# A chunked linear-attention and token-mixing kernel: values per unit, two transposes by DMA, decays as they are, one sum for X, another order

## The chip, the cores and the metric

The kernel runs on one core of one Trainium2 chip. A core has five engines that run beside each other: TensorE (PE), VectorE (DVE), ScalarE (ACT), GpSimd (POOL) and SyncE (SP), which here only issues DMA transfers. The metric is the device time of one execution in microseconds. Runs of the kernel before took 100.32 to 101.12 us, median 100.91 of 3.

## The reference

Inputs r, k, v, w have the shape (batch 4, heads 8, sequence 768, head size 48), u is 8 x 48. First a linear attention with a decay per channel, then a token mixer over the 384 channels of all heads:

```python
for t in range(S):                                   # for each batch and head
    cur = outer(u * k[t], v[t])
    y[t] = r[t] @ (state + cur)
    state = w[t][:, None] * state + outer(k[t], v[t])
# x: y with the heads side by side, (4, 768, 384)
wq = x @ w_q;  wk = x @ w_k                          # to 64 columns
W_tok = einsum('bsd,btd->bst', wq, wk) / 8
out = relu(einsum('bst,btd->bsd', W_tok, x)) @ w_out
```

## The kernel before

The sequence is cut into **units** of 256 positions, three to a batch, so there are 12 units, 0 to 11; units 9 to 11 are the last batch. A unit has two **chunks** of 128 positions, c = 0 and 1. Within a chunk the recurrence is done by matrix products: with the running product of the decays, r is multiplied by it (RT) and k divided by it (KT), the product of both, masked, gives the attention inside the chunk (AM), and a state per head (SB) carries over to the next chunk.

The program is a list of **steps**, each with a name, a unit and sometimes a chunk. For one unit they are, with the engine that can do them in brackets (E is PE, D is DVE, A is ACT, P is POOL, S is SP's DMA queue):

- wg, kg, rg, vg (S): the loads of w, k, r, v, 384 KB each.
- ln (A): logarithm of the decays. k16, r16, v16 (P, A or D): casts to bf16.
- cw (E): running sums of the logarithms. ep, en (A): their exponentials with plus and with minus.
- kT, rT (E): transposes of k and r. ks (A or D): kT copied out of PSUM. qT (D): rT times ks. RT (D): rT times ep. KT: ks times en, on POOL (P) or DVE (D), or straight from PSUM on DVE (written d).
- vp (E), VB (A or D): the values brought into the order of the partitions. dps (E), dd (A or D), Vd (P or D): the bonus term with u.
- A (E), AM (D): RT times KT for eight heads, then the mask. kb (E), kd (A or D): KT turned back.
- sn (E), SB (D): the new state. In form c the product goes out in two halves of 64 columns.
- yi, ya (E): y from the old state and from inside the chunk. X (D): y plus the bonus term, the row of the mixer's input.
- xt (E), XT (A or D): X transposed and copied out. qk (E), QK (A): X times w_q and w_k. In unit 11 X, xt, XT run per chunk, and qk is split into wq and wk with the copies wqc and wkc.

After the third unit of a batch: T (E), TS (A), the product of QK and X over the batch; then for each unit of the batch mx (E), rl (A or D, relu), fp (E, times w_out), os (A or D, copy out of PSUM) and st (a DMA store). The steps z are matmuls on zeros that keep PE's clock up; `WARM` counts them, and `setup` issues more before the first step.

The order of the steps over all engines is written out by hand in `ORDER` (found by a search), the engine of each step with a choice in `WAYS`, the PSUM banks in `BANKS`. Each engine does its own steps strictly in that order; a step waits by semaphores for those it depends on. Loads and stores are issued by SP in the same order, and a load waits until its buffer (`RINGS`, mostly 2 or 4 deep) is free.

Two things of the last batch differ from the others before the change. Its values are loaded at once for all three units (`WHOLE`, `load_whole`, the tile vw), in four transfers whose pieces are the 192 bytes of one position, straight into the right partitions; v16 and vp fall away there and VB is a cast from vw on POOL. And all decays are centred: a constant MU is taken off each logarithm, and the tables gx, gv, gk, IDU and a scaled mask US bring the factors back, in X, kd, sn and AM.

Of the kernel before, what the change touches and what calls it, by code (L numbers as in the profile page):

```python
# [142 lines left out]
def kernel(  # L143
# [81 lines left out]
    pos0 = const([C, 1], I32, "pos0")
    pos1 = const([C, 1], I32, "pos1")
    gx = const([C, 1], F32, "gx")
    gv = const([C, 1], F32, "gv")
    gk = const([C, 1], F32, "gk")
# [664 lines left out]
```

## Time and the profile before

| | |
|---|---|
| runs of the kernel before | 101.12, 100.32, 100.91 us (median 100.91) |
| the profiled execution | 101.37 us, of which the span of the trace is 99.6 |
| instructions in the span | 4492 |
| busy in the span | PE 86.6, DVE 84.9, ACT 79.0, POOL 69.5 us |
| moved by DMA | 24.68 MB, mean 248 GB/s |
| granted TensorE clock | 1.00 |

How the views are read: *busy* is the time in which an engine executes, without its waits. The view of stretches gives the busy time of each engine between two moments, the granted clock, the share of the DMA engines and what they moved. In the groups of instructions a line has the kernel's line, the engine, the operation, the tiles out<-in with their shapes, the count, the busy time in us and the mean of one in ns; behind the next bar the idle time of the engine just before these instructions, and what ended it. In the timeline each line begins with start and length in us. The chain that ended last is followed backwards from the last instruction, at each step to what released it. PSUM tiles all bear the name PS.

### The profile page before, as it was taken

How to read it: one execution, taken by the hardware profiler on the slowest of the kernel's cores; microseconds unless marked ns; L12 is line 12 of the kernel's file. 1: busy time of each engine (PE TensorE's matmuls, PEld its weight loads, DVE VectorE, ACT ScalarE, POOL GpSimd, SP SyncE). 2: the span in 40 equal slices, each digit the busy share in tenths (PEclk: the TensorE clock that was granted, in tenths of full speed). 3: DMA queues.
4: the chain of work that ended last, by engine and by line, in shares of the span. 5: the costliest groups of instructions: out<-in, count | busy, mean ns of one | idle time of the engine just before them, and what ended most of it. 6: DMA issues, size and time to landing. Idle time of an engine off the chain costs nothing.

```text
span 99.6 us, 4492 instructions
## 1 busy us (share of the span) xinstructions
PE 86.6 (87%) x1906; PEld 63.3 (64%) x1911; DVE 84.9 (85%) x154; ACT 79.0 (79%) x135; POOL 69.5 (70%) x82
## 2 busy tenths in 40 slices
PE   5978796879886998999999999889998999999930
PEld 1325473756774767777776777759787687776610
DVE  6284999799979999979999999999999799783740
ACT  6034998799996799899999998999899766666920
POOL 6866354999799895799999989498996392500000
PEclk9999999999999999999999999999999999999999
DMA  1999999799999999999999977998993056030794
GB/s 17 313 327 349 324 337 296 195 295 335 289 314 298 225 311 329 344 321 268 271 330 305 316 114 218 251 156 201 282 417 115 7 210 264 10 158 7 277 367 149
DMA packets 45141, 24.68 MB, mean 248 GB/s; under 512 B 31552, under 2 KB 43968, under 8 KB 45120
## 3 DMA queue, kind: packets, MB, share of 16 engines
q1 hardware_dynamic: 44960, 24.19, 84.0%
q8 instruction: 15, 0.25, 0.9%
q10 hardware_dynamic: 160, 0.20, 0.5%
q14 instruction: 6, 0.05, 0.1%
HBM read 19.66 MB, written 4.72 MB: 245 GB/s over the span
## 4 chain that ended last, share of the span: by engine, by line
PE 37%; DVE 23%; SPq 20%; DMA 7%; issue 7%; ACT 3%; ACTq 0%; DVEq 0%
PE PS L179 37%; SPq L232 9%; SPq L237 8%; DMA vg<-in_v_dram 7%; DVE AM L595 7%; DVE X L710 6%; DVE RT L516 3%; SPq L355 2%; DVE qT L506 2%; DVE ks L333 2%; DVE SB L658 1%; ACT VB L327 1%; SPq L357 1%; ACT MX L339 1%; DVE kd L335 1%
## 5 line engine op out<-in xcount | busy, mean ns | idle before, releaser
L595 DVE TENSOR_TENSOR AM<-PS,US 128x1024 bf16<-128x1024 f32 x24 | 28.8, 1218 | 0.7 <-PE PS L179 0.7
L526 POOL TENSOR_TENSOR KT<-ks,en 128x1024 bf16<-128x1024 bf16 (+1 forms) x10 | 19.7, 1965 | 4.7 <-DVE ks L333 3.3
L575 POOL TENSOR_TENSOR Vd<-VB,dd 128x768 bf16<-128x768 bf16 (+1 forms) x14 | 18.1, 1293 | 4.5 <-ACT dd L327 3.4
L454 ACT ACTIVATE en<-PS 128x1024 bf16<-128x1024 f32 (+1 forms) x14 | 12.5, 907 | 3.0 <-PE PS L179 2.9
L179 PEld LDWEIGHTS <-KT 48*128 48x128 bf16 (+1 forms) x312 | 9.7, 94 | 6.6 <-issue 4.5
L447 ACT ACTIVATE ep<-PS 128x512 bf16<-128x512 f32 (+1 forms) x28 | 13.7, 555 | 0.1
L179 PE MATMUL PS<-wo,MX 128*128 128x384 bf16 x72 | 13.5, 327 | 0.0
L710 DVE SCALAR_TENSOR_TENSOR X<-PS,gx,Vd 128x384 bf16<-128x384 f32 x22 | 12.5, 609 | 0.7 <-PE PS L179 0.6
L407 ACT ACTIVATE lw<-wg 128x768 bf16<-128x768 f32 x12 | 10.3, 857 | 2.9 <-DMA wg<-in_w_dram 2.9
L179 PE MATMUL PS<-RT,KT 48*128 48x128 bf16 x192 | 9.7, 218 | 1.2 <-ACT VB L327 0.4
L327 ACT COPY os<-PS 128x768 f32<-128x768 f32 (+1 forms) x11 | 7.9, 714 | 3.5 <-PE PS L179 3.5
L418 POOL CAST k<-kg 128x768 bf16<-128x768 f32 x10 | 8.3, 827 | 2.5 <-DMA kg<-in_k_dram 2.5
L179 PE MATMUL PS<-Z 128*128 128x512 bf16 x25 | 8.4, 461 | 1.4 <-DVE Z L250 1.2
L418 POOL CAST r<-rg 128x768 bf16<-128x768 f32 x10 | 8.2, 825 | 1.6 <-DMA rg<-in_r_dram 1.6
L179 PEld LDWEIGHTS <-MX 128*128 128x128 bf16 x72 | 6.5, 97 | 3.6 <-DVE MX L341 0.2
L516 DVE TENSOR_TENSOR RT<-PS,ep 128x1024 bf16<-128x1024 bf16 (+1 forms) x14 | 8.4, 605 | 0.0
L179 PE MATMUL PS<-VB,AM 128*128 128x48 bf16 x192 | 8.0, 184 | 0.4 <-issue 0.4
L506 DVE TENSOR_TENSOR qT<-PS,ks 128x1024 bf16<-128x1024 bf16 x12 | 8.2, 684 | 0.1
L339 ACT ACTIVATE MX<-PS 128x768 bf16<-128x768 f32 (+1 forms) x12 | 8.0, 682 | 0.4
L179 PE MATMUL PS<-CM,lw 64*128 64x128 bf16 x192 | 7.4, 217 | 0.5 <-DVE AM L595 0.3
L327 ACT CAST VB<-PS 128x768 bf16<-128x768 f32 x8 | 6.4, 804 | 1.1 <-PE PS L179 0.6
L179 PEld LDWEIGHTS <-AM 128*128 128x128 bf16 x192 | 6.3, 96 | 1.6 <-issue 0.7
(90 smaller groups left out, 191.9 us busy)
## 6 DMA issues: line engine op xcount, KB each, us to landing
kg<-in_k_dram SPq DMA_DIRECT2D x12, 384.0 KB, 6.4
wg<-in_w_dram SPq DMA_DIRECT2D x12, 384.0 KB, 5.0
rg<-in_r_dram SPq DMA_DIRECT2D x12, 384.0 KB, 5.8
vg<-in_v_dram SPq DMA_DIRECT2D x9, 384.0 KB, 6.3
out_dram<-os SPq DMA_DIRECT2D x9, 384.0 KB, 2.5
vw<-in_v_dram SPq DMA_DIRECT2D x4, 288.0 KB, 6.7
out_dram<-os SPq DMA_DIRECT2D x5, 192.0 KB, 2.4
wof<-in_moe_w_out_dram SPq DMA_DIRECT2D x1, 576.0 KB, 6.2
```

What stands on the lines that cost most here:

```text
L179: return nc.tensor.matmul(o, l, rr, start=start, stop=stop, skip_group_check=True, is_transpose=trans)
L327: nc.scalar.copy(o, i)
L407: nc.scalar.activation(view(lw.tile, 0, [[64, H], [512, 2], [1, D]]), view(g["wg"].tile, 0, [[D2, H], [D, 2], [1, D]]), ACT.Ln, bias=0.0, ...
L418: op(view(o.tile, 0, [[64, NP], [256, 4], [1, D]]), view(g[src].tile, 0, [[2 * D2, NP], [D, 4], [1, D]]))
L447: nc.scalar.activation(view(ep.tile, cs[0] * NP * EW + off, [[EW, NP * len(cs)], [step, 2], [1, 32]]), view(at(cw), cs[0] * 512 + j * 64, ...
L454: nc.scalar.activation(en.tile[:, ds(cs[0] * 512, w_)], at(cw)[:, ds(cs[0] * 512, w_)], ACT.Exp, bias=0.0, scale=-1.0)
L506: lambda e: nc.vector.tensor_tensor(plain(qT.tile), turned(512), plain(ks.tile), ALU.mult),
L516: nc.vector.tensor_tensor(plain(RT.tile, cs, 32), turned(512, cs, True), plain(ep.tile, cs, EW // 4), ALU.mult)
L526: x.tensor_tensor(KT.tile[:, cols], ks.tile[:, cols], en.tile[:, cols], ALU.mult)
L575: (nc.vector if e == "D" else nc.gpsimd).tensor_tensor(Vd.tile[:, cols], VB.tile[:, cols], view(dd.tile, cs[0] * H, [[1, len(cs) * H], [0, ...
L595: AMs[c] = add(("AM", n, c), "D", lambda e, c=c, A=A: nc.vector.tensor_tensor(view(AM[c].tile, 0, [[C, 8], [1, C]]), view(at(A), 0, [[C, 8 ...
L710: nc.vector.scalar_tensor_tensor(view(X.tile, 2 * i * DM + hh * D, [[D2, H], [1, D]]), view(at(y), hh * 512, [[D, H], [1, D]]), gx, view(V ...
```

## The change

- **Values.** The last batch's values are loaded, cast and brought in order per unit, as in the other batches (`WHOLE = ()`): three loads vg of 384 KB in place of four vw of 288 KB, three v16, three vp, and VB copied from PSUM.
- **Decays not centred.** MU, gx, gv, gk, IDU and the scaling of US go, with eight iotas and five small operations of the setup. kd becomes a plain copy; sn takes the identity.
- **X as one sum.** With gx gone, X of units 0 to 10 is one tensor_tensor of 768 columns in place of two scalar_tensor_tensor of 384. In unit 11 each of the two becomes a tensor_tensor.
- **XT of units 9 and 10 by DMA** (`TURN`). In place of xt (six 128x128 transposes, or twelve halves, on PE) and the copy XT, SP issues one DMA that transposes X from SBUF to SBUF (step xs). qk waits for it. The ring of XT gets a third buffer.
- **Order.** `ORDER`, `WAYS` and `BANKS` come from a new search. `begin` lets either of yi and ya come first. Three more z and three more warming matmuls in the setup.

```diff
@@ class Buf
+        self.begun = set()
+    def begin(self, part=None):
+        new = part not in self.begun
+        self.begun.add(part)
+        return new
...
-WARM = 12
+WARM = 15
+TURN = (9, 10)
...
-    WHOLE = (B - 1,)
-    SHIFT = 25
-    MU = -SHIFT * math.log(2.0) / C
-    UNIT = 2.0 ** -SHIFT
+    WHOLE = ()
...
-        SB=(4, NP * D, BF16), XT=(2, 2 * DM, BF16), ...
+        SB=(4, NP * D, BF16), XT=(3, 2 * DM, BF16), ...
...
@@ setup
-        for _ in range(18):
+        for _ in range(21):
             mm(PS[:, ds(0, 512)], Z[:, ds(0, C)], Z)
...
-            nc.gpsimd.iota(pos0[rows, :], ...)
-            nc.gpsimd.iota(pos1[rows, :], ...)
-        nc.scalar.activation(gx, pos0, ACT.Exp, bias=0.0, scale=MU)
-        nc.scalar.activation(gv, pos1, ACT.Exp, bias=0.0, scale=-MU)
...
-        nc.vector.tensor_scalar_mul(IDU, ID16, UNIT)
-        nc.vector.tensor_scalar_mul(gk, gv, UNIT)
-        nc.vector.tensor_scalar_mul(US, US, gv)
...
@@ ln
-                                 bias=0.0, scale=math.exp(-MU))
+                                 bias=0.0, scale=1.0)
@@ kd
-                copy(e, view(kd.tile, ...), x, gk)
+                copy(e, view(kd.tile, ...), x)
@@ sn
-                    mm(x[rows, ds(0, NP * D)], IDU[:, rows], old.tile, start=True, stop=False)
+                    mm(x[rows, ds(0, NP * D)], ID16[:, rows], old.tile, start=True, stop=False)
@@ X
-                for hh in range(2) if not end else ():
-                    nc.vector.scalar_tensor_tensor(
-                        view(X.tile, 2 * i * DM + hh * D, [[D2, H], [1, D]]),
-                        view(at(y), hh * 512, [[D, H], [1, D]]), gx,
-                        view(Vd.tile, hh * D, [[D2, H], [1, D]]), ALU.mult, ALU.add)
+                nc.vector.tensor_tensor(
+                    view(X.tile, 2 * i * DM, [[D, 2], [D2, H], [1, D]]),
+                    view(at(y), 0, [[512, 2], [D, H], [1, D]]),
+                    view(Vd.tile, 0, [[D, 2], [D2, H], [1, D]]), ALU.add)
@@ xt, XT
+            if n in TURN:
+                XTs = dma(("xs", n), lambda e, XT=XT: nc.sync.dma_start(
+                    out=view(XT.tile, 0, [[C, 2 * NK], [1, C]]),
+                    in_=X.tile[:, ds(2 * i * DM, 2 * DM)], transpose=True), [xs], XT, [X])
+            else:
+                XTs = add(("XT", n, c0), "AD", f_XT, [xts], XT, [xt], cols=DM * nc_)
```

What the new numbers mean, decoded into steps. **On another engine than before:** v16(3), uC, pads(0) from DVE to POOL; k16(1) from POOL to DVE; r16(0), r16(1) from POOL to ACT; k16(6), r16(9) from ACT to POOL; ks(1), XT(0), XT(8), os(7) from ACT to DVE; dd(0), dd(2), dd(3), kd(2), VB(7) from DVE to ACT, dd(9) the other way; KT(2), KT(3) and KT(11,0) from POOL to DVE, straight from PSUM; KT(0,0) on DVE straight from PSUM, KT(0,1) to POOL; Vd(6) from POOL to DVE; VB of units 9 to 11 from POOL to ACT; XT(9) (DVE) and XT(10) (ACT) gone. Of the output steps, rl(7), rl(8) go to ACT, and some os and rl of units 9 to 11 change sides. Five more sn take form c.

**First loads on SP:** before kg wg rg vg of unit 0, now wg kg rg vg; for units 3 to 5 before `wts wg3 wg4 kg3 rg3 kg4 vg3 kg5 rg4 rg5 vg4`, now `wg4 wg3 wts rg3 kg3 vg3 kg4 kg5 rg4 vg4 rg5`. **Last on SP:** before `rg11 st0 st2 st1 st4 st3 st5 st6 st7 ...`, now `rg11 st0 st2 st1 vg11 st3 xs9 xs10 st5 st6 st4 st7 ...`.

**On PE around the last AM:** before `A(11,0) A(11,1) yi(11,0) dps(11) fp(6) xt(10) yi(11,1) ya(11,0) ya(11,1) mx(7) qk(9) xt(11,0) qk(10) xt(11,1) wq(11,0) wk(11,0) mx(8) wk(11,1) T T T wq(11,1) fp(7) mx(9) fp(8) mx(10) fp(9) mx(11) fp(10) fp(11)`, now `A(11,0) A(11,1) yi(11,1) dps(11) fp(6) ya(11,0) mx(7) yi(11,0) ya(11,1) qk(9) xt(11,0) qk(10) xt(11,1) mx(8) wq(11,0) wk(11,0) wk(11,1) wq(11,1) T T T fp(7) mx(9) fp(8) fp(9,0) mx(10) mx(11) fp(9,1) fp(10) fp(11)`. **On DVE there:** before `RT(11,0) RT(11,1) X(10) SB(11,0) XT(9) AM(11,0) AM(11,1) X(11,0) X(11,1)`, now `RT(11,0) X(10) RT(11,1) SB(11,0) AM(11,0) AM(11,1) X(11,0) X(11,1)`.

More of the change, by code (lines that the diff above doesn't have):

```diff
@@ L82 @@
 ORDER = [
[40 rows of a table removed]
[41 rows of a table added]
 ]
 WAYS = (
-    "PDDDAPPDDdPADPPDDEEEAAPPAdPAAPEAcEEAAPPAPPADPeDEEDAAAAAAAAPPDPDADPeAcEEDAPPAdPAAPEAEEEDA"
-    "PPDPPAAPeAEEAAAAAAAAAAPDPPAAPEDEcEAAPPDPPDAPEAEEEAAPPDPPAAPeDceAAAAADADDPAAPPAPEDcEEDAPP"
-    "DPPAPeAcceAAPPDPPPAPPAEEDDAEDADAAADAAAADADDA"
+    "PPDPAPADdPPAAPPDDEEEDADADdPAAPEAEEEAAPPAdPAAPeAcEDAAAAAAAAPPDdPAAPeAccEDAPPAdPAAPEAccEDA"
+    "PPDPPAAPeAcEAAAAAAAAAPPDPPAADEDccEAAPPDPPAAPEAEEEAAPPDPPAAPeDceDAAAAADADPPAPPADPEDcEAPPD"
+    "PPAAPeAccAPPDdPPAAPPAEEDDAEDDDAAAADAAAADAAA"
 )
 BANKS = [
[6 rows of a table removed]
-]
-WARM = 12
[7 rows of a table added]
+]
+WARM = 15
+TURN = (9, 10)
 @with_exitstack
@@ L201 @@
         dd=(2, 2 * H, F32), Vd=(2, 2 * DM, BF16), AM0=(2, 1024, BF16), AM1=(2, 1024, BF16),
-        SB=(4, NP * D, BF16), XT=(2, 2 * DM, BF16), MX=(4, 2 * DM, BF16), X=(2, NCH * DM, BF16),
+        SB=(4, NP * D, BF16), XT=(3, 2 * DM, BF16), MX=(4, 2 * DM, BF16), X=(2, NCH * DM, BF16),
         QK=(2, QW, BF16), TS=(2, DM, BF16), vw=(2, NCH * DM, F32))
@@ L220 @@
     PM = const([C, C], BF16, "PM")
-    IDU = const([C, C], BF16, "IDU")
     Z = const([C, 512], BF16, "Z")
@@ L224 @@
     CM = const([C, 2 * C], BF16, "CM")
[L225 to L229, printed above, removed]
     def load(b, i, tl, ap):
@@ L257, in setup @@
                                                         ap=[[D2, NP], [1, D]]))
-        for q in range(4):
-            rows = ds(64 * (q % 2) + 32 * (q // 2), 32)
-            nc.gpsimd.iota(pos0[rows, :], pattern=[[0, 1]], base=q, channel_multiplier=4)
-            nc.gpsimd.iota(pos1[rows, :], pattern=[[0, 1]], base=q + 1, channel_multiplier=4)
-        nc.scalar.activation(gx, pos0, ACT.Exp, bias=0.0, scale=MU)
-        nc.scalar.activation(gv, pos1, ACT.Exp, bias=0.0, scale=-MU)
         nc.vector.memset(CM, 1.0)
@@ L619, in f_kd @@
                     x = view(at(kb, BF16), 0, [[C, n4], [64, 2], [1, D]])
-                copy(e, view(kd.tile, 64 + cs[0] * 1024, [[256, n4], [128, 2], [1, D]]), x, gk)
+                copy(e, view(kd.tile, 64 + cs[0] * 1024, [[256, n4], [128, 2], [1, D]]), x)
             x = add(("kd", n, cs[0]), "AD", f_kd, [x] + ([wts["pads"][n]] if n < 2 else []), kd,
@@ L667, in of, with f_yi @@
             return at(ys[c])[:, ds(h * D if end else h % 2 * 512 + (c * NP + h // 2) * D, D)]
-        def f_yi(e, c, start):
+        def f_yi(e, c):
+            start = ys[c].begin()
             heads = [(hp, hh) for hp in range(NP) for hh in range(2)]
@@ L678, in f_yi, with f_ya @@
                    start=(start and hp == 0 and not (end and hh)), stop=False)
-        def f_ya(e, c, start):
+        def f_ya(e, c):
+            start = ys[c].begin()
             for h in range(H):
@@ L687, in y_add @@
             yas[c] = add(("ya", n, c), "E",
-                         lambda e, c=c, x=ys[c].filler is None: f_ya(e, c, x), [AMs[c], VBs], ys[c],
+                         lambda e, c=c: f_ya(e, c), [AMs[c], VBs], ys[c],
                          [AM[c], VB])
@@ L694, in unit @@
                 yis[c] = add(("yi", n, c), "E",
-                             lambda e, c=c, x=ys[c].filler is None: f_yi(e, c, x),
+                             lambda e, c=c: f_yi(e, c),
                              [RTs[c], oldss[c]], ys[c], [RT, olds[c]], mode=1)
@@ L706, in unit, with f_x @@
             y = ys[c0]
-            def f_x(e, c0=c0, nc_=nc_, y=y):
-                for hh in range(2) if not end else ():
-                    nc.vector.scalar_tensor_tensor(
-                        view(X.tile, 2 * i * DM + hh * D, [[D2, H], [1, D]]),
-                        view(at(y), hh * 512, [[D, H], [1, D]]), gx,
-                        view(Vd.tile, hh * D, [[D2, H], [1, D]]), ALU.mult, ALU.add)
-                if end:
-                    nc.vector.scalar_tensor_tensor(
-                        X.tile[:, ds((2 * i + c0) * DM, DM)], at(y)[:, ds(0, DM)], gx,
-                        Vd.tile[:, ds(c0 * DM, DM)], ALU.mult, ALU.add)
+            def f_x(e, c0=c0, y=y):
+                if end:
+                    nc.vector.tensor_tensor(X.tile[:, ds((2 * i + c0) * DM, DM)],
+                                            at(y)[:, ds(0, DM)], Vd.tile[:, ds(c0 * DM, DM)],
+                                            ALU.add)
+                    return
+                nc.vector.tensor_tensor(
+                    view(X.tile, 2 * i * DM, [[D, 2], [D2, H], [1, D]]),
+                    view(at(y), 0, [[512, 2], [D, H], [1, D]]),
+                    view(Vd.tile, 0, [[D, 2], [D2, H], [1, D]]), ALU.add)
             xs = add(("X", n, c0), "D", f_x,
@@ L720, in unit @@
                      X, [y, Vd], cols=DM * nc_)
-            xt, XT = either(), ring("XT")
+            xt, XT = None if n in TURN else either(), ring("XT")
             def f_xt(e, c0=c0, nc_=nc_, xt=xt):
@@ L734, in f_xt @@
                                X.tile[rows, x], ID16[rows, rows], trans=True)
-            xts = add(("xt", n, c0), "eE", f_xt, [xs], xt, [X], cols=nc_, mode=dict(e=1, E=0))
+            if n not in TURN:
+                xts = add(("xt", n, c0), "eE", f_xt, [xs], xt, [X], cols=nc_, mode=dict(e=1, E=0))
             def f_XT(e, nc_=nc_, xt=xt, XT=XT):
@@ L753, in f_wk, with f_wq @@
                     for kt in range(NK):
-                        mm(at(qk)[:, ds(k0 + k_ * DH, DH)], XT.tile[:, ds(kt * nq + k_ * C, C)],
+                        mm(at(qk)[:, ds(k0 + k_ * DH, DH)], XT.tile[:, ds((k_ * NK + kt) * C if n in TURN else kt * nq + k_ * C, C)],
                            wk_sb[:, ds(kt * DH, DH)], start=(k_ == 0 and kt == 0),
                            stop=(kt == NK - 1))
-            def f_wq(e, nq=nq, wq=wq, XT=XT):
+            def f_wq(e, nc_=nc_, nq=nq, wq=wq, XT=XT):
                 for kt in range(NK):
                     mm(at(wq)[:, ds(0, nq)], wq_sb[:, ds(kt * C, C)],
-                       XT.tile[:, ds(kt * nq, nq)], start=(end and kt == 0),
+                       view(XT.tile, kt * C, [[NK * C, nc_], [1, C]]) if n in TURN
+                       else XT.tile[:, ds(kt * nq, nq)], start=(end and kt == 0),
                        stop=(kt == NK - 1))
@@ L793, in f_T @@
                 ii, c = divmod(gi, 2)
+                start = T.begin(c)
                 mm(at(T)[ds(c * DH, DH), ds(0, DM)], QK.tile[:, ds(ii * QS + U + c * DH, DH)],
-                   X.tile[:, ds(gi * DM, DM)], start=(gi < 2), stop=(gi >= NCH - 2))
+                   X.tile[:, ds(gi * DM, DM)], start=start, stop=(gi >= NCH - 2))
         parts = [list(range(4)), [4], [5]] if end else [list(range(NCH))]
```

1 line of the change is left out of this document (removed), and 94 rows, old and new, of tables (BANKS, ORDER).

## The prediction

> **What bounds the kernel now.** I read the page from the top: span, engine sums, the chain that ended last by engine.
>
> ```profile
> span 99.6 us, 4492 instructions
> ...
> PE 86.6 (87%) x1906; PEld 63.3 (64%) x1911; DVE 84.9 (85%) x154; ACT 79.0 (79%) x135; POOL 69.5 (70%) x82
> ...
> PE 37%; DVE 23%; SPq 20%; DMA 7%; issue 7%; ACT 3%; ACTq 0%; DVEq 0%
> ```
>
> No engine owns the whole span. The sums are close together, so they must be read stretch by stretch. I cut at events: 12.62 us is the start of the first AM (step AM(0,0)), 85.57 us the end of the last one (AM(11,1)).
>
> ```profile
> core 0: us, PE busy (x) PEld busy (x) DVE busy (x) ACT busy (x) POOL busy (x), PEclk, DMA share, GB/s
> 12.62:30.00 17.38, 14.42 (x396) 11.43 (x395) 15.95 (x27) 16.15 (x25) 14.10 (x15) 1.00 1.02 293
> 30.00:50.00 20.00, 18.34 (x464) 14.14 (x462) 19.45 (x32) 17.99 (x29) 17.93 (x16) 1.00 1.04 297
> 50.00:65.00 15.00, 14.32 (x376) 11.01 (x371) 15.00 (x25) 14.64 (x25) 13.02 (x12) 1.00 0.99 253
> 65.00:76.36 11.36, 11.10 (x284) 8.94 (x285) 11.17 (x18) 10.85 (x20) 11.05 (x10) 1.00 0.91 252
> 76.36:85.57 9.21, 8.54 (x191) 6.07 (x188) 8.35 (x15) 5.84 (x13) 4.82 (x6) 1.00 0.35 134
> 85.57:89.47 3.90, 3.90 (x67) 3.17 (x68) 2.85 (x7) 2.73 (x6) 0.55 (x1) 1.00 0.26 101
> ```
>
> Three parts. From 12.62 to 30.00 DVE stands idle for 1.43 us, and DMA engines are full: the loads set the pace. From 30.00 to 85.57 DVE is idle for 0.55 + 0.00 + 0.19 + 0.86 = 1.60 us of 55.57: DVE is the bound (53.97 busy, 97%), with PE at 94% (52.30) and ACT at 89% (49.32) close behind. After 85.57 PE is busy without a gap, and the chain of waits stays on it to the last output copy:
>
> ```profile
> 21.53 7.07 DMA vg<-in_v_dram
> ...
> 85.56 10.02 PE PS L179 x107
> ```
>
> The first line is the load of unit 3's values, which ends at 28.60. DVE waited 0.73 us for it, and then cast it:
>
> ```profile
> 28.62 1.31 DVE L333 CAST v<-vg 128x768 bf16<-128x768 f32 x1 [0.73 <-DMA vg<-in_v_dram]
> ```
>
> **The change part by part.** I decoded the old and new orders into steps and give each exchanged step the duration of its group.
>
> ```profile
> L595 DVE TENSOR_TENSOR AM<-PS,US 128x1024 bf16<-128x1024 f32 x24 | 28.8, 1218 | 0.7 <-PE PS L179 0.7
> L658 DVE TENSOR_TENSOR SB<-PS,ep 128x192 bf16<-128x192 f32 x20 | 7.0, 349 | 0.0
> L333 DVE COPY ks<-PS 128x1024 bf16<-128x1024 bf16 x8 | 5.5, 685 | 1.7 <-PE PS L179 1.7
> L333 DVE COPY XT<-PS 128x768 bf16<-128x768 bf16 x4 | 2.2, 550 | 0.0
> L521 DVE TENSOR_TENSOR KT<-PS,en 128x1024 bf16<-128x1024 bf16 x2 | 1.4, 678 | 0.0
> L335 DVE TENSOR_SCALAR kd<-PS,gk 128x768 bf16<-128x768 bf16 x2 | 1.2, 608 | 0.0
> L333 DVE CAST VB<-PS 128x768 bf16<-128x768 f32 x1 | 0.9, 949 | 0.0
> L333 DVE COPY dd<-PS 128x16 f32<-128x16 f32 x3 | 0.5, 163 | 0.0
> L521 DVE TENSOR_TENSOR KT<-PS,en 128x512 bf16<-128x512 bf16 x1 | 0.4, 411 | 0.0
> ```
>
> *X as one sum.* Two operations of 384 columns become one of 768 in units 0 to 10. Start to start is what counts, since neighbours on DVE overlap a little:
>
> ```profile
> 57.62 0.36 DVE L658 TENSOR_TENSOR SB<-PS,ep 128x192 bf16<-128x192 f32 x1
> 57.89 0.68 DVE L506 TENSOR_TENSOR qT<-PS,ks 128x1024 bf16<-128x1024 bf16 x1
> 58.49 1.13 DVE L710 SCALAR_TENSOR_TENSOR X<-PS,gx,Vd 128x384 bf16<-128x384 f32 x2
> 59.54 0.68 DVE L516 TENSOR_TENSOR RT<-PS,ep 128x1024 bf16<-128x1024 bf16 x1
> ```
> ```profile
> 25.82 1.22 DVE L595 TENSOR_TENSOR AM<-PS,US 128x1024 bf16<-128x1024 f32 x1
> 26.95 0.68 DVE L333 COPY ks<-PS 128x1024 bf16<-128x1024 bf16 x1
> ```
>
> The pair holds DVE for 59.54 - 58.49 = 1.05 us. A tensor_tensor that reads f32 from PSUM, as the new sum does, holds it for 0.27 at 192 columns (57.89 - 57.62) and 1.13 at 1024 (26.95 - 25.82). The line through both gives 0.27 + 576 x 0.00103 = 0.87 at 768, an estimate. Bounds: 0.55 (the XT copy of 768 bf16) and 1.13 (AM). Each X saves 0.18, between 0.50 and -0.08.
>
> *DVE up to some 30 us* (units 0 to 2). Off it: dd(0), dd(2), dd(3) 0.49, kd(2) 0.61, v16(3) 1.31, three X 0.54: 2.95. Onto it: ks(1) 0.69, KT(2) and KT(3) straight from PSUM 1.36, XT(0) 0.55: 2.60. Net -0.35. The wait of 0.73 for unit 3's values can shrink: their load moves ahead of kg(4) in the queue, and POOL casts it. I take 0.3 of the 0.73. Ahead of 12.62 the loads land as before; uC and pads(0) leave DVE and uT no longer stands ahead of kT(0) on PE, but k16(1) joins DVE there (between the other exchanges' 0.55 and v's 1.31). I cost that at nothing, from -0.9 to +0.7. The constants dropped from the setup (iotas, gx, gv, gk, IDU, the scaling of US) stood while everything waited for the first loads: nothing. The three warming matmuls more lie under the same wait, and the three z fill PE gaps that the stretch 12.62:30 shows (14.42 busy of 17.38). Part one: -0.65.
>
> *DVE from 30 us to the last AM.* Off it: VB(7) 0.95, XT(9) 0.55, eight X 1.44. Onto it: XT(8) 0.55, dd(9) 0.16, KT(11,0) 0.41, Vd(6). Vd(6) has no row on DVE; its bounds are 0.55 (copy of 768) and 1.31 (cast of 768 from SBUF), and I take 0.95, the cast of 768 in between. kd without its factor becomes a plain copy, 0.61 to 0.55, in three places: -0.17. Net -3.11 + 2.07 = -1.04; two instructions more that overlap by 0.08 each: -1.2. The 1.60 us of idle time I leave as they are.
>
> *Values of units 9 to 11 as in the other units.* POOL casts three v16 instead of three VB, PE gains three vp, and ACT gains three VB copies:
>
> ```profile
> L327 ACT CAST VB<-PS 128x768 bf16<-128x768 f32 x8 | 6.4, 804 | 1.1 <-PE PS L179 0.6
> L327 ACT COPY XT<-PS 128x768 bf16<-128x768 bf16 x7 | 5.6, 800 | 1.1 <-PE PS L179 1.1
> ```
>
> That is 2.41 us on ACT between about 65 and 76, against XT(8) and a dd of about 0.16 that leave it (0.96): +1.4 where ACT has 11.36 - 10.85 = 0.51 left. I cost it at nothing because most steps there wait for DVE; the rival below drops that. The loads get cheaper: vw in 54 to 66 us went in 192-byte pieces at 253 GB/s, when the stretch before moved 297. DMA is no bound there.
>
> *XT of units 9 and 10 by DMA.* PE loses both xt, DVE and ACT one XT copy each (counted). What comes in is a wait: qk(9) and qk(10) on PE for the transposes. Behind qk(10) on PE stand xt(11,1), wq, wk, T and all output matmuls; behind xs(9) and xs(10) on SP stand the stores of units 5, 6 and 4. os(8) needs the buffer that unit 4's store frees, but it comes only after T, mx(9) and fp(8).
>
> ```profile
> 81.44 1.14 DVE L710 SCALAR_TENSOR_TENSOR X<-PS,gx,Vd 128x384 bf16<-128x384 f32 x2
> 83.23 2.34 DVE L595 TENSOR_TENSOR AM<-PS,US 128x1024 bf16<-128x1024 f32 x2
> 86.24 1.14 DVE L715 SCALAR_TENSOR_TENSOR X<-PS,gx,Vd 128x384 bf16<-128x384 f32 x2 [0.67 <-PE PS L179]
> ```
> ```profile
> out_dram<-os SPq DMA_DIRECT2D x5, 192.0 KB, 2.4
> vw<-in_v_dram SPq DMA_DIRECT2D x4, 288.0 KB, 6.7
> ```
> ```profile
> 62.99 2.61 SPq L243 DMA_DIRECT2D vw<-in_v_dram  x1
> ```
> ```profile
> 82.00 0.50 PE L179 MATMUL PS<-ID,X 128*128 128x128 bf16 x6
> ```
>
> The cover of xs(10): X(10) ends at 82.58, the last AM at 85.57. In between XT(9) goes (0.55) and RT(11,1) comes (about 0.35): 2.8. X(11,0), half of 1.14, and its xt (some 0.35) follow before qk(10): 3.7 us in all. No row shows a transposing DMA. By the nearest by size and by the quiet queue, a 192 KB store, it lands 2.4 us after its issue; the slowest row is 6.7, and with the longest issue of one transfer in the queue 2.61 + 6.7 = 9.3. I take 2.4: hidden, 1.3 to spare. Unit 9 has a whole unit more. The Trainium skill (VectorE: DVE Perf Modes, sections The three transpose paths and Rules for kernel authors) speaks against the change: it gives 1309 ns for one 128x128 block by DMA and 390 on TensorE, and advises TensorE where PSUM will do. The trace has PE faster still, six blocks in 0.50 us. Six blocks one after another would be 7.9 us, an estimate from that page; by it the sum would be 4.2 us worse.
>
> *The end.* After the last AM the old order has ya(11,0), ya(11,1), mx(7) before qk(9), and DVE waited 0.67 for X(11,0). In the new one only ya(11,1) is left there: yi(11,0), ya(11,0) and mx(7) can run under the AM. X(11,0) can start at once. From there PE runs the same work, dense as before. I take -0.5, between -0.7 and 0.
>
> **Sum:** -0.65 - 1.2 - 0.5 = -2.35, so 97.25 for the span. The profiled execution took 101.37 (span 99.6 and 1.77 around it), which gives 99.0; it lies 0.46 above the median of 100.91. Against the median: 98.6.
>
> **The rivals.** *ACT takes over* in 65 to 76 us: +1.4 of work against 0.51 of room, 0.9 over, which eats most of DVE's gain: 99.5. For it: ACT at 95% there, and en and ep of unit 11 stand behind VB(11). Against: DVE is fuller still. *The transposes come late.* One mechanism, one place: PE stands at qk(10). It costs from 3.7 us after X(10) on, one for one. At 6.7 it is +3.0, 101.6; at 9.3 it is +5.6, 104.2. It decides the sign at 3.7 + 2.3 = 6.0 us. By the Trainium skill's figure above (VectorE: DVE Perf Modes) it would be 7.9 and 102.8, an estimate. For it: no row shows such a DMA, and the two loads quoted took 6.7 and 7.07 us. Against: those had a full queue; here DMA is at 0.35. *Better packing*: the new order closes the 1.60 us of DVE's idle time after 30 us: 97.0. For it: 0.86 of it lies in one place, 76 to 86, where PE work is taken away. *X does not get cheaper*, at AM's 1.13: 11 x 0.26 back = +2.9: 101.5. Against it: AM has 256 columns more.
>
> **How the numbers follow.** Forecast 0.47 (97.5 to 99.8), ACT 0.20 (99.0 to 100.3), late transposes 0.13 (100.5 to 104), packing 0.14 (96.0 to 97.5), X 0.06. Differences within 1% (99.9 to 101.9) can hardly be told from no change here. Faster by over 1%: 0.46 + 0.12 + 0.14 = 0.72. Slower by over 1%: 0.09 of the late transposes. Same: 0.19. The range 96.8 to 101.4 leaves out under a tenth at each end; the unknown X and the start lie within it.
>
> **What would show it.** X as one instruction of about 0.95 us; DVE's last AM ending near 83.7; PE without a wait at qk(10) and the transposes landing within 3.7 us; 12 VB on ACT without DVE waiting for ACT in 65 to 76; X(11,0) starting right behind the last AM. Wrong if PE waits for a DMA ahead of T, or if DVE's idle time after 30 us grows beyond 2.5 us.

## The result, and the profile after

The changed kernel took 105.84 us (median of 6, 103.91 to 106.42) beside 101.03 of the kernel before (6 runs, 100.32 to 102.26): ratio 1.034, 95% interval 1.026 to 1.043. It is slower; the prediction was 98.6, faster. A second set of runs of the same kernel (*same*, below) gave 106.63 and 1.042 (1.029 to 1.055). The profiled execution took 105.49, of which the span is 103.8. Ratios take the fast runs of each kernel alone and medians take all; the profiled executions of the changed kernel (105.49 beside 103.91 for its fastest) and of *shift63*, *shift21*, *whole_new*, *old_to_x6* and *old_to_x8* below are slow ones, so their lengths show where time goes and the ratios show how much.

First the page of the changed kernel: span, engine sums, the chain by engine.

```profile
span 103.8 us, 4481 instructions
...
PE 89.0 (86%) x1909; PEld 64.8 (62%) x1915; DVE 81.9 (79%) x136; ACT 80.6 (78%) x138; POOL 65.0 (63%) x74
...
PE 57%; DVE 23%; ACT 10%; issue 5%; DVEq 0%; ACTq 0%
```

DVE has 3.0 us less to do, as intended, and the span is 4.2 longer: the saved time became waits, and the chain runs on PE for 57% instead of 37%. Where? I cut both spans at the starts of X(0), X(4), X(6), X(8) and X(11). Before:

```profile
core 0: us, PE busy (x) PEld busy (x) DVE busy (x) ACT busy (x) POOL busy (x), PEclk, DMA share, GB/s
19.32:45.38 26.06, 22.89 (x594) 17.99 (x592) 24.81 (x40) 23.67 (x37) 23.09 (x21) 1.00 1.04 304
45.38:58.49 13.11, 12.74 (x323) 9.79 (x318) 13.07 (x23) 13.04 (x21) 12.57 (x12) 1.00 1.05 288
58.49:68.78 10.29, 9.47 (x273) 7.36 (x271) 10.29 (x17) 9.93 (x18) 8.74 (x7) 1.00 0.90 175
68.78:86.24 17.46, 16.79 (x388) 12.99 (x385) 15.75 (x27) 13.65 (x27) 12.74 (x12) 1.00 0.58 204
86.24:99.60 13.36, 9.32 (x91) 6.41 (x88) 6.81 (x13) 6.81 (x16) 0.00 (x0) 1.00 0.47 178
```

And after:

```profile
19.35:48.31 28.96, 24.57 (x613) 18.98 (x616) 24.66 (x36) 24.09 (x40) 18.67 (x20) 0.94 1.00 288
48.31:62.34 14.03, 12.68 (x325) 9.80 (x320) 13.47 (x20) 13.47 (x21) 13.97 (x13) 1.00 1.07 315
62.34:72.36 10.02, 9.12 (x271) 7.25 (x269) 9.95 (x15) 9.39 (x16) 9.47 (x9) 1.00 0.94 292
72.36:90.02 17.66, 17.50 (x383) 13.03 (x380) 15.76 (x26) 14.81 (x28) 10.67 (x10) 1.00 0.27 70
90.02:103.80 13.78, 9.12 (x92) 6.15 (x89) 5.25 (x11) 7.18 (x16) 0.00 (x0) 0.99 0.54 202
```

The differences are +2.90, +0.92, -0.27, +0.20 and +0.42 us. In the first stretch DVE's work is the same (24.81 and 24.66) and its idle time grows from 1.25 to 4.30 us. The granted clock is 0.94 there. The timeline of the changed kernel, PE and then DVE, and the stretches behind show why:

```profile
28.07 0.61 PE L184 MATMUL PS<-CM,lw 64*128 64x128 bf16 x16
28.52 0.26 PE L184 MATMUL PS<-SB,RT 48*128 48x48 bf16 x7
31.04 0.28 PE L184 MATMUL PS<-SB,RT 48*128 48x48 bf16 x9 [2.27 <-issue]
```
```profile
32.60 0.96 DVE L706 TENSOR_TENSOR X<-PS,Vd 128x768 bf16<-128x768 f32 x1 [1.78 <-POOL r L408]
34.58 0.69 DVE L511 TENSOR_TENSOR KT<-PS,en 128x1024 bf16<-128x1024 bf16 x1 [1.02 <-PE PS L184]
```
```profile
30.00:32.00 2.00, 0.96 (x27) 0.88 (x27) 0.83 (x2) 0.79 (x1) 0.95 (x2) 0.99 1.02 299
32.00:34.00 2.00, 2.00 (x29) 1.20 (x28) 0.96 (x1) 0.96 (x2) 0.61 (x1) 0.50 0.95 248
34.00:36.00 2.00, 1.96 (x54) 1.50 (x50) 1.15 (x2) 1.14 (x3) 0.94 (x1) 0.66 0.94 254
```

PE stands for 2.27 us in the middle of a step: seven of the 16 matmuls of yi(2) are done, the other nine wait for no engine and no transfer ("issue"). DVE runs dry behind it, waiting 1.78 and 1.02 us, and then PE's clock is granted at 0.50 and 0.66 for four microseconds. The page has a DMA queue that carries instructions, q8, which I take to be PE's (the last section gives the count). One packet of it passed in each kernel shortly before such a stop; the rows are the queue's in 28.4 to 28.7 (changed) and what PE had done up to there, and then the same for 26.2 to 26.5 (before):

```profile
q8 instruction: 1, 0.02, 23.3%
...
0.00:28.40 28.40, 23.68 (x463) 15.94 (x469) 21.34 (x46) 20.27 (x34) 18.21 (x33) 1.00 0.97 277
```
```profile
q8 instruction: 1, 0.02, 20.0%
...
0.00:26.20 26.20, 21.12 (x409) 13.36 (x413) 21.06 (x52) 18.61 (x31) 18.93 (x39) 1.00 0.98 280
```

The kernel before has a stop at the same count, the 480th weight load, and a short one:

```profile
28.75 0.21 PE L179 MATMUL PS<-VB,AM 128*128 128x48 bf16 x2 [0.40 <-issue]
...
0.00:28.75 28.75, 23.02 (x476) 14.97 (x480) 22.89 (x55) 20.94 (x35) 20.86 (x41) 1.00 0.99 281
```

In both PE went on some 2.3 to 2.6 us after the packet. Before, it came with 67 weight loads left to the 480th, after with 11, and so PE stood longer. **Theory F:** PE ran out of instructions, because a block came late. **Theory O:** the new order loses by its own waits, and the stop is a feature of that step. **Theory V:** the values per unit load ACT and PE.

### The profile page after: what moved, and what is told of

Its sections match the earlier page's. It is cut to its first block, busy times and chain, and to the rows that moved or that the text cites. A ratio compares the mean times of both kernels' runs of the same rounds, so it can differ in the third digit from the quotient of the medians.

```text
span 103.8 us, 4481 instructions
## 1 busy us (share of the span) xinstructions
PE 89.0 (86%) x1909; PEld 64.8 (62%) x1915; DVE 81.9 (79%) x136; ACT 80.6 (78%) x138; POOL 65.0 (63%) x74
## 4 chain that ended last, share of the span: by engine, by line
PE 57%; DVE 23%; ACT 10%; issue 5%; DVEq 0%; ACTq 0%
PE PS L184 57%; DVE AM L585 9%; ACT ep L437 3%; DVE RT L506 3%; DVE X L706 3%; DVE qT L496 2%; ACT en L444 2%; DVE ks L323 2%; DVE SB L648 2%; DVE KT L511 1%; DVE XT L323 1%; ACT ks L317 1%; ACT os L317 1%; ACT lw L397 1%; ACT VB L317 1%
## 5 line engine op out<-in xcount | busy, mean ns | idle before, releaser
L565 POOL TENSOR_TENSOR Vd<-VB,dd 128x768 bf16<-128x768 bf16 (+1 forms) x13 | 16.5, 1279 | 8.6 <-ACT dd L317 7.3
L516 POOL TENSOR_TENSOR KT<-ks,en 128x1024 bf16<-128x1024 bf16 (+1 forms) x8 | 15.1, 1888 | 6.6 <-DVE ks L323 5.4
L323 POOL CAST v<-vg 128x768 bf16<-128x768 f32 x12 | 10.6, 888 | 2.7 <-DMA vg<-in_v_dram 2.7
L706 DVE TENSOR_TENSOR X<-PS,Vd 128x768 bf16<-128x768 f32 x11 | 10.5, 953 | 1.9 <-POOL r L408 1.8
L184 PE MATMUL PS<-Z 128*128 128x512 bf16 x30 | 9.7, 448 | 1.4 <-DVE Z L249 1.2
L329 ACT ACTIVATE MX<-PS 128x768 bf16<-128x768 f32 (+1 forms) x14 | 9.5, 697 | 1.1 <-PE PS L184 0.9
L317 ACT CAST VB<-PS 128x768 bf16<-128x768 f32 x12 | 9.5, 804 | 0.6 <-POOL wk L357 0.2
L323 DVE COPY ks<-PS 128x1024 bf16<-128x1024 bf16 x9 | 6.1, 681 | 4.5 <-PE PS L184 4.5
L184 PE MATMUL PS<-VB,AM 128*128 128x48 bf16 x192 | 8.7, 185 | 0.2 <-issue 0.2
```

Of the source, the lines that this page charges most:

```text
L184: return nc.tensor.matmul(o, l, rr, start=start, stop=stop, skip_group_check=True, is_transpose=trans)
L317: nc.scalar.copy(o, i)
L323: x.tensor_copy(o, i)
L516: x.tensor_tensor(KT.tile[:, cols], ks.tile[:, cols], en.tile[:, cols], ALU.mult)
L565: (nc.vector if e == "D" else nc.gpsimd).tensor_tensor(Vd.tile[:, cols], VB.tile[:, cols], view(dd.tile, cs[0] * H, [[1, len(cs) * H], [0, ...
L706: nc.vector.tensor_tensor(view(X.tile, 2 * i * DM, [[D, 2], [D2, H], [1, D]]), view(at(y), 0, [[512, 2], [D, H], [1, D]]), view(Vd.tile, 0 ...
```

## The experiments

Kernels are built from the changed one; "old" is the order, engines, banks and warming of the kernel before. Starts of X in the profiles (us):

| kernel | X(0) | X(4) | X(6) | X(8) | X(9) | X(11) | span |
|---|---|---|---|---|---|---|---|
| before | 19.32 | 45.38 | 58.49 | 68.78 | 75.82 | 86.24 | 99.6 |
| changed | 19.35 | 48.31 | 62.34 | 72.36 | 80.15 | 90.02 | 103.8 |
| old_order | 19.47 | 44.29 | 58.04 | 68.16 | 75.17 | 84.92 | 98.7 |
| turn_old | 19.05 | 44.29 | 57.15 | 67.62 | 74.63 | 84.24 | 98.8 |
| per_unit_old | 20.32 | 45.95 | 58.89 | 69.00 | 78.65 | 89.69 | 103.5 |
| old_start | 19.25 | 44.47 | 59.39 | 69.42 | 77.21 | 87.07 | 100.9 |
| shift63 | 20.51 | 46.33 | 60.37 | 71.75 | 79.55 | 89.42 | 103.2 |
| three_back | 20.32 | 46.28 | 59.91 | 70.75 | 78.48 | 88.22 | 101.8 |
| new_to_x4 | 19.92 | 47.37 | 62.03 | 72.16 | 79.15 | 88.49 | 101.7 |

### same, old_order, old_start, pe_xt: which part loses

```diff
 # old_order
-ORDER, WAYS, BANKS, WARM of the changed kernel; WHOLE = (); TURN = (9, 10)
+those of the kernel before; WHOLE = (B - 1,); TURN = ()
 # old_start: the first 344 steps, up to X(4), in the old order on the old engines
 # pe_xt
-TURN = (9, 10)
+TURN = ()      # xt and XT of units 9, 10 back in the order
```

Expected of *same*:

> The changed kernel again, nothing altered, for a second profile. Theory F (instruction fetch): PE stood 2.27 us before its 480th weight load at 28.8 us, in the middle of a step and with no wait of that instruction, because the packet with its next instructions went through the full DMA queues only at 28.6 us; the gap is a matter of chance, so this profile shows a gap of another length (0.4 to 3 us) at the same weight load, always about 2.4 us after that packet, and the span follows the gap; median 104 to 106. Theory O (order): the new order itself makes the engines wait between 20 and 45 us; X(4) starts at 48.3 again whether the gap is there or not.

Of *old_order*:

> Only decays not centred and X as one sum; order, engines, banks, loads, warming matmuls all as before the change. The working of the prediction: eleven X save 0.18 each and some kd 0.06, most of it while DVE is the bound: 98.9 to 99.6 against 101. Rival: the freed DVE time turns into waits for loads or for PE, 100.3 to 101.2. Theory F allows either; its gap at the 480th weight load should stay as short as before the change, 0.4 us or so.

Of *old_start*:

> The changed kernel, but its first 344 steps, up to X(4), in the old order and on the old engines; from there on the new order. X(4) started at 45.4 before the change and at 48.3 after it. If what was lost lies in the start (theory O for the start, or theory F, since the gap was 0.40 with the old start), the time is 101.0 to 102.5. If the later part loses as much by itself, it stays above 103.5.

Of *pe_xt*:

> The changed kernel, but XT of units 9 and 10 again by transposes on PE and a copy on DVE and ACT, put where the old order had them. If the DMA transposes cost (PE waiting at qk(9) or qk(10)), this is faster than the changed kernel by over 1 us. If they are hidden, it is 0 to 1 us slower, as DVE and ACT get 0.55 and 0.80 of work back in a stretch that both fill.

Measured: *same* 106.63, 1.042 (above); PE stops there for 1.78 us at the same weight load, some 2.6 us after a packet of q8, and X(4) starts at 47.94. *old_order* 102.40, ratio 0.999 (0.993 to 1.005). *old_start* 104.62, ratio 1.019 (1.007 to 1.030). *pe_xt* 107.10, ratio 1.057 (1.049 to 1.065). So neither the sum X nor the decays cost anything, and they bring nothing that can be told from no change. The loss is in the order and what came with it, a part of it before X(4). The DMA transposes are worth some 1.5 to 2.3% in the new order (X(9) to X(11) takes 9.87 us in the changed kernel, 11.71 in *pe_xt*): the step of the prediction that they are hidden holds.

### shift63, shift21, old_loads: is it the block of instructions?

```diff
 # shift63 (shift21: range(42), 256 columns)
-        for _ in range(21):
-            mm(PS[:, ds(0, 512)], Z[:, ds(0, C)], Z)
+        for _ in range(84):
+            mm(PS[:, ds(0, 128)], Z[:, ds(0, C)], Z[:, ds(0, 128)])
 # old_loads: the first 26 loads in the old order on SP
```

Of *shift63*:

> The changed kernel with its 21 warming matmuls of 512 columns cut into 84 of 128 columns: the same columns, but 63 more weight loads ahead of the first step, so that every later PE instruction has another place in PE's instruction stream; steps, engines and loads as in the changed kernel. Theory F (PE stood 2.27 us inside yi of unit 2, ahead of its 480th weight load, because its next block of instructions had not come): no gap at that yi any more; if there is one it lies again ahead of about the 480th weight load, which is now 63 loads earlier in the work, and its length is another. With the gap gone X(2) starts near 30.5 instead of 32.6 and the profiled time falls to 102 to 104; if a later block meets a dense stretch, the gap moves and the time stays above 104.5. Theory O (the new order's own waits and transfers): the gap stays in yi of unit 2, 1.3 to 2.3 us long, and the median stays at 105.5 to 107.

Of *shift21*:

> The changed kernel with its 21 warming matmuls of 512 columns cut into 42 of 256: 21 more weight loads ahead of the first step, all else the same. With 63 more the gap of 2.27 us inside yi of unit 2 was gone. Theory F (blocks of instructions come late): the gap, if PE still runs dry, lies again ahead of about the 480th weight load, so 21 loads earlier in the work than in the changed kernel, in the step before yi or in an earlier one, and is between 0 and 2.3 us long; the time lies between 103.8 and 106. Against F: the gap stays inside yi of unit 2 behind 7 of its matmuls, wherever that is in the count (about the 501st).

Of *old_loads*:

> The changed kernel with its first 26 loads issued in the order of the kernel before (kg(0) first, the weights of the mixing part ahead of unit 3's); everything else, the compute steps included, as in the changed kernel. Theory F with the DMA engines' backlog as its cause: POOL's wait for the weights (1.63 us) goes, the lull of the DMA share at 20 to 22 us (0.74) fills, PE's third block of instructions comes less than 2 us after the 370th weight load instead of 3.4, the gap in yi of unit 2 shrinks below 0.8, X(4) starts near 46 instead of 48.3, and the median is 103 to 104. Theory O (the compute order alone loses the start): X(4) stays at 47.5 or later and the median at 105.5 or more. The loads could also come too late for the new compute order, which takes wg(4) early: then DVE or ACT waits for a DMA in the first 25 us.

Measured: *shift63* 103.82, ratio 1.025 (1.020 to 1.030); *shift21* 104.41, 1.022 (1.015 to 1.029); *old_loads* 104.94, 1.033 (1.025 to 1.040). In *shift63* yi(2) runs through:

```profile
29.68 0.36 PE L184 MATMUL PS<-SB,RT 48*128 48x48 bf16 x16
29.98 0.37 PE L184 MATMUL PS<-VB,AM 128*128 128x48 bf16 x8
```

In *shift21* PE stops again, now inside another step (cw, after 2 of 16) and again with 479 weight loads done:

```profile
29.32 0.22 PE L184 MATMUL PS<-CM,lw 64*128 64x128 bf16 x2
30.26 0.57 PE L184 MATMUL PS<-CM,lw 64*128 64x128 bf16 x14 [0.72 <-issue]
...
0.00:30.26 30.26, 24.81 (x475) 18.79 (x479) 21.95 (x47) 20.41 (x34) 18.73 (x33) 1.00 0.96 275
```

The stop follows the count of instructions and not the step. The packets say the same: the profiles of all kernels here have 17 stops of 0.6 us or more marked "issue", and in each of them PE goes on 2.3 to 2.7 us after a packet of q8; in *shift63*, which has none, the packet passed some 2.6 us ahead of the 480th weight load. That decides for F as the cause of the stop. Whether the new order also loses by its own waits (O) is not decided by it. *old_loads* kept the stop (0.94) and had another (1.49 at 41.47): the old order of loads does not take it away, and its time cannot be told from the changed kernel's.

### turn_old, per_unit_old: the other parts in the old order

```diff
 # turn_old: old_order with
-TURN = ()
+TURN = (9, 10)       # xs right behind X(9), X(10)
 # per_unit_old: old_order with
-WHOLE = (B - 1,)
+WHOLE = ()           # v16 on POOL, vp on PE, VB on ACT for units 9 to 11
```

Of *turn_old*:

> The order, engines, banks, loads and warming of the kernel before, values of the last batch loaded whole, with three of the five edits: decays not centred, X one sum, and XT of units 9 and 10 by DMA transposes right behind X(9) and X(10). Without the transposes this order took 102.4 beside 101.6 before (ratio 0.999). If the transposes are worth what they were in the new order (107.1 without, 105.8 to 106.6 with them): about 1 us less, 100 to 101.2, ratio 0.985 to 0.992, with X(11) to the end falling from 10.22 to about 9.6. If what they free is idle anyway: 0.995 to 1.003. If qk(9) or qk(10) waits for a transpose: above 1.005, with PE waiting for a DMA ahead of T.

Of *per_unit_old*:

> The order, engines, loads and warming of the kernel before with three of the five edits: decays not centred, X one sum, and the values of the last batch loaded per unit (v16 of units 9 to 11 cast on POOL, permuted by three more groups of 4 matmuls on PE, VB copied by ACT out of PSUM in place of POOL's copies). Without the third it took 102.4 (ratio 0.999). PE gets about 3 x 0.8 us more, ACT 3 x 1.0 us, POOL about the same. If PE and ACT have the room, as the prediction took it: 0.995 to 1.005. If it is on the path of the later part (X(4) to the end was 0.6 to 1.8 us longer in the new order): 1.008 to 1.025, with X(9) to X(11) later by 1 to 2 us and DVE's waits for PE grown there.

Measured: *turn_old* 102.91 (100.63 to 104.13) beside 101.45 (100.58 to 103.58): no verdict. Its profile starts X(11) at 84.24 and ends only 0.8 us before that of the kernel before. I had hoped for a version that beats both; it is not shown to be one. *per_unit_old* 104.34, ratio 1.032 (1.026 to 1.039): the values per unit cost three per cent in the old order, more than expected. X(8) to X(9) takes 9.65 us there, against 7.01 in *old_order*. PE waits for VB on ACT:

```profile
71.86 1.14 PE L182 MATMUL PS<-wo,MX 128*128 128x384 bf16 x6 [0.90 <-ACT VB L315]
...
79.81 0.62 PE L182 MATMUL PS<-CM,lw 64*128 64x128 bf16 x16 [1.02 <-ACT VB L315]
```

This is the rival *ACT takes over*, and theory V holds in that order, with the added steps where I put them. In the new order X(8) to X(9) is 7.79 (7.04 before), with dd(9) and XT(8) on DVE instead of ACT:

```profile
74.32 0.17 DVE L323 COPY dd<-PS 128x16 f32<-128x16 f32 x1
...
75.37 0.56 DVE L323 COPY XT<-PS 128x768 bf16<-128x768 bf16 x1 [0.28 <-PE PS L184]
```

### vd_pool, whole_new, three_back: causes of the later loss, put back one by one

Behind X(4) the largest item is the product Vd(6), now on DVE, and PE's wait for the copy ks that stands behind it:

```profile
58.99 1.64 DVE L565 TENSOR_TENSOR Vd<-VB,dd 128x768 bf16<-128x768 bf16 x1
60.55 0.68 DVE L323 COPY ks<-PS 128x1024 bf16<-128x1024 bf16 x1
```
```profile
61.29 0.41 PE L184 MATMUL PS<-PM,r 64*128 64x64 bf16 x16 [1.03 <-DVE ks L323]
```

```diff
 # vd_pool: one letter in WAYS
-Vd(6): D
+Vd(6): P
 # whole_new
-WHOLE = ()
+WHOLE = (B - 1,)     # VB of units 9 to 11 on POOL; order else as changed
 # three_back: shift63, vd_pool and whole_new together
```

Of *vd_pool*:

> The changed kernel with one letter changed: the product Vd of unit 6 on POOL as in the kernel before, instead of on DVE, where it took 1.64 us (the prediction had 0.95). X(5) to X(6), 9.85 us against 8.74 before, falls to 8.7 to 9.3, with PE's wait of 1.03 for ks of unit 8 gone; the median falls by 0.5 to 1.1 us from the changed kernel's 105.8 to 106.6. If DVE's 1.64 us was time in which DVE would have waited anyway: no change in X(5) to X(6), and the median stays. If POOL is late with Vd: X(6) waits for POOL.

Of *whole_new*:

> The changed kernel with the last batch's values loaded whole again, as four transfers, and VB of units 9 to 11 on POOL; v16 and vp of these units gone. Order else as in the changed kernel. In the old order the values per unit took the ratio from 0.999 to 1.032. If they cost the new order too: X(8) to X(9) falls from 7.8 to 7.0 to 7.3 and the median by 0.6 to 1.2 us, to 104.7 to 105.4. If the new order has room for them (the prediction's reading): the median stays at 105.6 to 106.8. If the pieces of 192 bytes come late for VB(9): POOL waits for a DMA and X(9) is later.

Of *three_back*:

> The changed kernel with three things together: the warming cut into 84 matmuls (shift63, which took 103.8 by itself), Vd of unit 6 on POOL, the last batch's values whole. If the three causes add up: 105.8 - 2.1 - 1.0 - 0.8 = about 102, within 1% of the kernel before, with X(4) near 46.3, X(5) to X(6) near 8.8 and X(8) to X(9) near 7.1. If they hide one another: 103 to 104. If another block of PE's instructions comes late in the shifted stream, a wait of PE on no other engine shows in the middle of a step and the time is above 103.

Measured: *vd_pool* 105.71, ratio 1.034 (1.028 to 1.041), as the changed kernel. X(5) to X(6) falls from 9.85 to 9.23, and X(6) to X(7) grows from 5.35 to 6.41: POOL is now late with KT, and PE and DVE wait for it in turn.

```profile
63.09 0.27 PE L183 MATMUL PS<-ID,KT 48*128 48x48 bf16 x8 [1.02 <-POOL KT L515]
```
```profile
63.41 0.36 DVE L322 COPY kd<-PS 128x384 bf16<-128x384 bf16 x1 [1.04 <-PE PS L183]
```

*whole_new* 106.61, ratio 1.029 (1.021 to 1.037): no gain that can be told from no change. X(8) to X(9) is 8.04; dd(9) and XT(8) stayed on DVE there. *three_back* 104.23, ratio 1.021 (1.015 to 1.028), against 1.025 of *shift63* alone. Two of the three causes that I had named thus bring nothing clear of noise when they are put back alone; in *vd_pool* the wait moved to another engine.

### new_to_x4, old_to_x6, old_to_x8: where the rest lies

```diff
 # new_to_x4: new order up to X(4) with the warming of shift63, old order behind
 # old_to_x6, old_to_x8: old order up to X(6), X(8), new order behind
 # in all three the values whole, XT of units 9, 10 by DMA
```

Of *new_to_x4*:

> The new order and engines up to X(4), with the warming cut into 84 matmuls so that PE's blocks of instructions fall elsewhere (as in shift63), the old order and engines from there; values whole, XT of units 9 and 10 by DMA, decays not centred, X one sum. If the new start is at fault only through the late block of instructions: X(4) near 46.3 and 0.99 to 1.008. If the new start loses by its own waits too (X(4) at 46.3 in shift63 against 44.3 in the old order): 1.01 to 1.025, X(4) at 46 or later with no gap in the middle of a PE step.

Of *old_to_x6*:

> Old order and engines up to X(6), the new ones from there; the last batch's values whole, XT of units 9 and 10 by DMA, decays not centred, X one sum. Old up to X(4) with the new rest gave 1.019, the old order throughout 0.999 (without the transposes). Theory M (the middle loses: Vd of unit 6 on DVE and what stands around it, X(4) to X(6) 14.03 in the changed kernel against 13.11): 0.995 to 1.008, since X(4) to X(6) is the old stretch. Theory L (the last third loses: XT(8), dd(9) on DVE, X(8) to X(9) 7.8 against 7.0): 1.012 to 1.025.

Of *old_to_x8*:

> Old order and engines up to X(8), the new ones from there; else as in old_to_x6. Theory M: as old_to_x6, 0.99 to 1.005, with X(8) near 67.6 to 68.8 and X(8) to the end near 31.2. Theory L: if the loss lies behind X(8), 1.01 to 1.02 here too; if it lies between X(6) and X(8), this one is 0.99 to 1.005 and old_to_x6 over 1.01.

Measured: *new_to_x4* 104.07, ratio 1.016 (1.010 to 1.023). *old_to_x6* 104.53, 1.028 (1.022 to 1.034); *old_to_x8* 106.15, 1.034 (1.026 to 1.042). The last two say nothing of M and L: in the profile of *old_to_x6* the old start itself lost 4 us (X(4) at 48.48; DVE waits 1.1 us for a load, and PE's clock is granted at 0.50 from 33 to 39 us), and in *old_to_x8* ACT waits 2.3 us for a load of the seam. *new_to_x4* has a stop of PE that no shift had shown, 128 weight loads further on, so it, too, leaves open whether the new start loses by its own waits:

```profile
32.16 0.19 PE L182 MATMUL PS<-UB,qT 128*128 128x2 bf16 x2
33.84 0.29 PE L182 MATMUL PS<-UB,qT 128*128 128x2 bf16 x6 [1.49 <-issue]
...
0.00:33.84 33.84, 27.13 (x603) 22.55 (x607) 25.31 (x51) 23.93 (x40) 21.33 (x36) 1.00 0.98 276
```

Set beside each other, the profiles with the new start show what the stops cost. The count is that of weight loads done.

| kernel | stops of PE before X(4) of 0.6 us or more (count) | X(0) to X(4), us |
|---|---|---|
| changed | 2.27 (479) | 28.96 |
| pe_xt | 1.33 (479), 1.22 (735) | 28.90 |
| whole_new | 1.90 (480), 0.94 (735) | 27.81 |
| same | 1.78 (479), 0.88 (735) | 27.69 |
| new_to_x4 | 1.49 (607) | 27.45 |
| old_loads | 0.94 (479), 1.49 (735) | 27.40 |
| shift21 | 0.72 (479) | 26.85 |
| vd_pool | 0.86 (479), 0.61 (735) | 26.50 |
| three_back | none | 25.96 |
| shift63 | none | 25.82 |

Without a stop the new start takes 25.8 to 26.0 us; the old one took 26.06 in the kernel before and 24.82 in *old_order*. Beside the kernel before, the stops are thus all that the start lost, up to 3 us in a profile. But the old order with the same X and decays takes 24.8 to 25.2 us (*old_order*, *old_to_x8*, *old_start*, *turn_old*), so that the new start is 0.6 to 1.1 us longer even without a stop; no run shows why. From X(4) to the end the old order with its values whole takes 54.2 to 54.5 us (before, *old_order*, *turn_old*, *new_to_x4*), the new one 55.2 to 57.8 (*old_loads* and *whole_new* are the ends).

## Why the prediction was wrong

- **X as one sum**: right. 953 ns as one instruction, and 0.86 from start to start (62.34 to 63.20), where I had taken 0.87:

```profile
62.34 0.95 DVE L706 TENSOR_TENSOR X<-PS,Vd 128x768 bf16<-128x768 f32 x1
63.20 0.68 DVE L506 TENSOR_TENSOR RT<-PS,ep 128x1024 bf16<-128x1024 bf16 x1
```

- **Transposes hidden**: right. qk(10) starts behind xt(11,0) without a wait, 4.8 us after X(10) ended (85.06 + 0.96, from DVE's timeline); where exactly they land the trace does not say.

```profile
85.06 0.96 DVE L706 TENSOR_TENSOR X<-PS,Vd 128x768 bf16<-128x768 f32 x1
...
86.93 2.36 DVE L585 TENSOR_TENSOR AM<-PS,US 128x1024 bf16<-128x1024 f32 x2 [0.31 <-PE PS L184]
90.02 1.02 DVE L702 TENSOR_TENSOR X<-PS,Vd 128x384 bf16<-128x384 f32 x2 [0.73 <-PE PS L184]
```
```profile
90.64 0.34 PE L184 MATMUL PS<-ID,X 128*128 128x128 bf16 x3
90.81 0.34 PE L184 MATMUL PS<-wk,XT 128*128 128x64 bf16 x6
```

The sum came out at +4.2 for the span in place of -2.35: 2.93 up to X(4), 0.79 from there to the last AM, 0.48 behind it.

- **Part one, -0.65**: X(2) starts 1.55 us later (32.60, 31.05) and X(4) 2.93. The step that failed is the premise "the loads set the pace" with PE's gaps as free room ("the three z fill PE gaps"): PE stood 2.27 us in the middle of a step where it had stood 0.40, and DVE's idle time from X(0) to X(4) rose by 3.05 us, while its work fell by only 0.15. The profile of before showed "issue" as 7% of the chain, and its stop of 0.40; I quoted the first and did not ask what it was. F is shown as the mechanism of the stop; by the runs it is worth 0.9 to 2.0% (1.034 and 1.042 against 1.025 and 1.022, with intervals that overlap in part), a quarter to a half of the loss. The forecast gain is not there without a stop either: see the 0.6 to 1.1 us above.
- **Part two, -1.2**: wrong by 2.0; from X(4) to the end of the last AM the changed kernel takes 40.98 us (48.31 to 89.29) against 40.19 (45.38 to 85.57). Two terms failed. Vd(6) on DVE took 1.64, not 0.95. And "the 1.60 us of idle time I leave as they are": between X(4) and X(11) DVE's idle time went from 1.75 to 2.53 us, while its busy time went from 39.11 to 39.18. What left DVE there (seven sums X 1.26, VB(7) 0.95, XT(9) 0.55) is 2.76 us, what came (Vd(6) 1.64, XT(8) 0.56, dd(9) 0.17, KT(11,0) 0.41) is 2.78. The prediction had named an idle time after 30 us above 2.5 us as a sign of being wrong; from 30 us to the last AM it was 5.60 us. Why idle time grew behind X(4) is only partly shown: one cause put back (*vd_pool*) came back as a wait for POOL.
- **The end, -0.5**: wrong by 1.0. X(11,0) did not start at once but 0.73 us behind the last AM, 0.67 before: PE, which has no gap there, reaches yi(11,0) and ya(11,1) only when the last AM ends at 89.29.

```profile
89.30 0.62 PE L184 MATMUL PS<-SB,RT 48*128 48x48 bf16 x8
89.84 0.37 PE L184 MATMUL PS<-VB,AM 128*128 128x48 bf16 x8
```

The rest of the miss is behind the work. The last output copies (os, the first line before, the second after) end at 96.12 and 99.66, so X(11,0) to there became 0.24 us shorter (9.88 to 9.64); from there to the end of the span, with only stores under way, it is 4.14 us in place of 3.48. The sum had no term for that.

```profile
95.64 0.48 ACT L327 COPY os<-PS 128x384 f32<-128x384 f32 x1 [0.98 <-PE PS L179]
```
```profile
97.74 1.92 ACT L317 COPY os<-PS 128x384 f32<-128x384 f32 x4
```

- **Values per unit at nothing**: not so in the old order, where they cost 3%. In the new one *whole_new* (1.029) cannot be told from the changed kernel, so their price there is not shown.
- **The rivals**: "ACT takes over" was seen only in *per_unit_old*, "late transposes" nowhere. X did get cheaper, and DVE's idle time grew instead of closing. None of the rivals was what decided: I had none in which PE itself becomes late.

What stays open: why the block of instructions comes later in the new order, and which waits make that order 0.6 to 1.1 us longer before X(4) and 1 to 3 us longer behind it. The DMA engines were full in both. PE had done 352 weight loads, one step of 128 before the stop, at 23.8 us before and 24.5 after; the packet passed some 2.5 and 4.0 us later, so that the delay is more in the packet than in PE's pace.

## What to carry to other kernels

A saving on the busiest engine is a gain only if what feeds it gets there earlier too; count the feeder's time, not its "gaps". In a profile, look at idle time marked "issue" in the middle of a step: if its place follows the instruction count, shift the instructions by some more of them ahead, as *shift63* did, before reordering the work. And test the old order with the same steps before crediting the parts of a change: here X as one sum and the plain decays were neutral in it (0.999), the values per unit lost 3%, and the kernels in the new order lost 2 to 4%.
